# First weights of the first expert loaded through GpSimd's queue at step 16 and split in steps 17 to 19; four table scatters put behind tile 23's decayed queries

## The chip, the cores and the metric

The kernel runs on one core of a Trainium2 chip. The core has a matrix engine (TensorE, PE in the profile; PEld is its loading of weights), VectorE (DVE), ScalarE (ACT), GpSimd (POOL) and SyncE (SP, which only issues transfers), and 16 DMA engines that all queues share. Each engine works through its own instructions in program order and stops at an instruction whose semaphores are not yet there. The metric is the time of one execution in microseconds (us) on the device.

## What is computed

A retention layer over 4 batches, 8 heads, 768 positions and 64 channels a head, then a mixture of 8 experts with one expert for each token:

```python
for b in range(nb):                       # blocks of 64 positions, per batch and head
    intra = (qb @ kb.T * Dmask) @ vb      # Dmask: lam ** (i - j) below the diagonal
    inter = (qb * lam_pow) @ kv_state
    out[b] = intra + inter
    kv_state = lam_block * kv_state + (kb * rev_pow).T @ vb
x = out.transpose(0, 2, 1, 3).reshape(3072, 512)
e_idx = argmax(x @ w_gate)                # one expert of 8 for each token
h  = relu(x[mask] @ w1[e])                # 512 -> 1024, float32
ye = h @ w2[e]                            # 1024 -> 512
out[mask] = gate_w * sigmoid(x @ w_output_gate)[e] * ye
```

## The kernel before

**Attention.** The 3072 tokens are 24 tiles of 128 positions (6 chunks by 4 batches). A software pipeline runs over steps s = -2 to 21. Step s transposes the queries and keys of tile s+2 (`stage_a`: PSUM banks pk and pq, L341), applies the running state to the decayed queries of tile s (`stage_c1`, L424), makes the scores of tile s+1 (`stage_b`, L400) and multiplies the scores of tile s by its values and updates the state (`stage_c`, L441 and L454). ScalarE copies the transposed keys and queries out of PSUM (kT L344, qT L345) and the outputs (xT L448). VectorE applies the decay to the scores (L409), updates the state (L466) and turns the outputs for their store (xn L532). GpSimd makes the decayed queries (`stage_q`, qd, L375; in two halves for tiles 20 to 23) and decayed keys (kd, L316). All PSUM tiles share 8 banks, so a new tile of PSUM waits for the engine that reads the old tile of its bank.

**Routing.** For every four tiles logits are made, and for each token a record (row, scale) is scattered to a table in HBM by GpSimd, one indirect DMA for a tile (`place_scatter`, L679). In the last steps the order of GpSimd's work is written by hand in the dictionary `work`, whose three lists for a step are run between the halves of `stage_q`, ahead of the decayed keys, and behind them. The expert that is largest after 12 tiles is taken first; its rows of the first 12 tiles are gathered in steps 17 to 19 (`row`, L900). A later load of the table index (L834) waits until all scatters ahead of it have landed.

**Experts.** Float32 weights come in pieces of 1 MB (`load_piece`, L119, tile raw with 3 buffers, issued by SP) and are split in two parts: whi, a cast on ScalarE (`split_hi`, L132), and wlo, the rest, on VectorE (`split_lo2`, L146 for two quarters at once), for three matmuls per product (`mm3`, L85 to L87). Piece 0 is the first half of the first expert's w1. Behind the last step the program goes on with tiles 22 and 23, `keep_places`, the first expert's first columns (`x_hi`, `x_lo`), the logits of the last four tiles, and then `fill`, which runs matmuls of the first expert while the rest of its rows are still being routed. From about 144 us on the experts follow one another.

Of the kernel before, what the change touches and what calls it, by code (L numbers as in the profile page):

```python
# [23 lines left out]
def kernel(  # L24
# [13 lines left out]
    nc = tc.nc  # L38
# [37 lines left out]
    RES = 16  # L76
# [33 lines left out]
    def load_piece(i, eng=nc.sync, j=None):  # L110
        if i >= len(pieces):
            return
        p, m, s = pieces[i]
        src = (w1, w2)[m][bass.ds(expert[p], 1)]
        src = src[:, :, s * HALF : (s + 1) * HALF] if m == 0 else src[:, s * HALF : (s + 1) * HALF, :]
        if i not in raws:
            raws[i] = wpool.tile([P, 4, 512], F32, tag="raw", bufs=3, name=f"raw_{i}")
        c = slice(0, 4) if j is None else slice(j, j + 1)
        eng.dma_start(raws[i][:, c, :], src.rearrange("e (c p) f -> p (e c) f", p=P)[:, c, :])  # L119

    def split_hi(i, j):
        if i >= len(pieces):
            return
        if pieces[i] not in wparts:
            wparts[pieces[i]] = (
                wpool.tile([P, 4, 512], F32R, tag="whi", bufs=4, name=f"whi_{i}"),
                wpool.tile([P, 4, 512], F32R, tag="wlo", bufs=4, name=f"wlo_{i}"),
            )
        src, hi = raws[i][:, j, :], wparts[pieces[i]][0][:, j, :]
        if turned_out(i):  # L130
            src, hi = by_quarter(src), by_part(hi)
        nc.scalar.copy(out=hi, in_=src)  # L132
# [10 lines left out]
    def split_lo2(i, h):  # L143
        sl = slice(2 * h, 2 * h + 2)
        hi, lo = (t[:, sl, :] for t in wparts[pieces[i]])
        nc.vector.tensor_tensor(out=lo, in0=raws[i][:, sl, :], in1=hi.bitcast(F32), op=ALU.subtract)  # L146
# [149 lines left out]
    def blank_rows():  # L296
        norow = wpool.tile([P, E * EB * 3], I32, tag="raw", bufs=3, name="norow")
        nc.gpsimd.memset(norow, NOROW)
        nc.sync.dma_start(tab_d.rearrange("(p r) t -> p (r t)", p=P), norow)
# [132 lines left out]
    def stage_c(n):  # L432
        L = live[n]
        c, b = divmod(n, B)
        vt = qkv[n][2]
        xT = slot(f"xT_{n}")
        for y in range(2):
            po = L["po"][y]
            for m in range(4):
                i, j = divmod(m, 2)  # L440
                nc.tensor.matmul(  # L441
                    po[j * D : (j + 1) * D, i * P : (i + 1) * P],
                    vt[:, 4 * y + m, :],
                    L["at"][y][:, m, :],
                    start=(c == 0),
                    stop=(c == 0 or m >= 2),
                )
            nc.scalar.copy(out=xT[:, 256 * y : 256 * y + 256], in_=po[:, 0:256])  # L448
        L["xT"] = xTs[n] = xT
        if c < NCH - 1:  # L450
            pst = bank(f"pst_{n}")
            for m in range(4):
                for y in range(2):
                    nc.tensor.matmul(  # L454
                        pst[y * D : (y + 1) * D, m * D : (m + 1) * D],
                        L["kd"][:, 2 * m + y, :],
                        vt[:, 4 * y + m, :],
                        start=True,
                        stop=True,
                    )  # L460
            psv = pst[:, 0 : 4 * D].rearrange("p (m d) -> p m d", m=4)
            if c == 0:
                nc.vector.tensor_copy(out=state[b], in_=psv)
            else:
                for m in range(4):
                    nc.vector.scalar_tensor_tensor(  # L466
                        out=state[b][:, m], in0=state[b][:, m], scalar=qdec[:, m, P - 1 : P], in1=psv[:, m],
                        op0=ALU.mult, op1=ALU.add,
                    )
            weave()  # L470
            weave()
# [356 lines left out]
    def load_rows(p, j0=0, j1=None, eng=nc.sync):  # L828
        if p >= E:
            return  # L830
        n = (KT[p] if j1 is None else j1) - j0
        t = const.tile([32, 4, n, 3], I32, name=f"index_{p}_{j0}")
        src = tab_v[bass.ds(expert[p], 1)][:, :, j0 : j0 + n, :]
        eng.dma_start(t, src.rearrange("e (b r) j t -> (e r) b (j t)", b=4))  # L834
        idxs[(p, j0)] = (t, n)
# [381 lines left out]
    with tc.manual_schedule():  # L1217
# [12 lines left out]
        def row(b):  # L1230
            return lambda: gather(0, b, b + 1, RES0 * P)

        def rec():
# [5 lines left out]
            RES0: ([], [], []),  # L1239
            RES0 + 2: ([], [rec], [rec]),  # L1240
            RES0 + 3: ([], [rec], [rec, lambda: load_rows(0, 0, 2, nc.gpsimd)]),
            RES + 2: ([row(2)], [], [row(3)]),
            RES + 3: ([row(4)], [], [row(5)]),
            RES + 4: ([rec], [], [rec]),
            RES + 5: ([rec], [], [rec]),
        }
        between.update({(s, k): fs for s, w in work.items() for k, fs in zip(("q", "qk", "end"), w)})

        for s in range(-2, NTILE - 2):
            if s >= 0:  # L1250
                load_up_to(s + AHEAD - (4 <= s <= RES), 2 if s <= RES else 1)
            for i in range(3):
                if s == RES + (2, 4, 5)[i]:
                    load_piece(i)
            if s == -2:
                decay_table()
            if s == 0:
                stage_b(1)
                stage_b2(1)
            rest = stage_a(s + 2)  # L1260
            if late and s != RES + 5:
                late.pop(0)()
            if s >= 1 and s % B == 0:
                logits(s - B, B)
            for f in rest:
                f()
            if s >= 0:
                stage_c1(s)
            stage_a2(s + 2)
            if s == RES + 4:  # L1270
                stage_q(s + 2)
            if s + 1 >= 0 and s != 0:
                stage_b(s + 1)
            if s == RES + 5:
                late.pop(0)()
                seen = rank_counts("plater")
            n = s - 1
            if s >= 1 and s % B == 0:
                logit_rows(s - B)
            if n >= 0 and n % B == B - 1:  # L1280
                choice = route_choose(n + 1 - B, n + 1)
                ranking = route_place(n + 1 - B, n + 1)
                if s != RES + 4:
                    at_once(choice)
                    pace(uncounted[-1][0][0:1, 0, 0:1])
                per_turn[0] = 3 if n >= RES else 2
            if s == RES + 5:
                stage_d2(LAST)
            if s + 1 >= 0 and s != 0:
                stage_b2(s + 1)  # L1290
            stage_k(s + 2)
            if s == RES0 + 2:
                expert_regs(0, order_i, 1)
            if s == RES + 5:
                for f in held[:6]:
                    f()
                x_turn(0, 0)
            gap_work(s, "end")
            if s == RES + 4:
                at_once(choice[:-1])  # L1300
            if 0 <= n < LAST:
                stage_d2(n)
            if s == 0:
                later.extend(inter_tables())
                routing_tables()
                order_tables()
            if s == 1:
                weave(len(later))
            if s == 2:
                blank_rows()  # L1310
            if s >= 0:
                stage_c(s)
            if s == RES + 4:
                choice[-1]()
            if s == RES + 1:
                row_index(0)
                row(0)()
                row(1)()
            if ranking and s == RES + 4:
                late.append(ranking[0])  # L1320
                held = ranking[1:]
                ranking = []
            if ranking and s != RES0:
                late.append(ranking[0])
                later.extend(ranking[1:])
                ranking = []
            if ranking:
                for f in pick_first():
                    f()
                late.append(ranking[0])  # L1330
                later.extend(ranking[1:])
                ranking = []
            if s < RES0 - 2:
                place_scatter(1)

        n = NTILE - 1
        for j in range(2):
            split_hi(0, j)
        stage_c1(n - 1)
        stage_b(n)  # L1340
        stage_b2(n)
# [8 lines left out]
            x_hi(0, g, 0)  # L1350
        for g in range(NPAIR):
            x_lo(0, g, 0)
        split_lo2(0, 0)
        split_hi(0, 2)
        load_piece(3)
        stage_c1(n)
        stage_c(n)
        split_hi(0, 3)
        split_lo2(0, 1)
        for i in range(2):  # L1360
            rows_of(LAST + i)
        logits(LAST, B)
# [249 lines left out]
```

## Time and profile before

| | |
|---|---|
| median of 3 runs | 418.16 us (417.45 to 418.74) |
| the profiled execution | 415.14 us |
| its span, first to last instruction | 413.4 us |
| PE / PEld busy | 400.8 us (97%) / 367.1 us (89%) |
| DVE / POOL / ACT busy | 286.7 / 238.8 / 190.4 us |
| HBM traffic | 190 GB/s over the span |

The timeline gives for each group of instructions the start, the duration, the engine, the line, the operation with its tiles, and in brackets the idle time of the engine just before with what ended it. The windows give the busy time of each engine in a stretch, the granted clock of TensorE (1.00 is 2.4 GHz, 0.50 is 1.2 GHz), the busy share of the DMA engines, and GB/s. A DMA instruction's duration is its issue, not its transfer.

### The profile page before, as it was taken

To read this page: it belongs to the slowest core of one execution; us is meant where nothing else is said; L and a number is where in the kernel's file an instruction comes from. 1 tells how busy PE (TensorE), PEld (TensorE's weight loads), DVE (VectorE), ACT (ScalarE), POOL (GpSimd) and SP (SyncE) were. 2 spreads that over 40 slices of the span, in tenths; PEclk is the share of its full clock that TensorE was granted. 3 is DMA by queue.
4 is the path that set the end of the run, shared out by engine and by line. 5 is a ranking of instruction groups with operands and counts; after the bars stand their busy time and mean duration, and the time that the engine had idled before them with its cause. 6 is when DMAs were issued, how large, how long until landed. Compare 5 with 4: busy or idle time off the path is not lost.

```text
span 413.4 us, 10570 instructions
## 1 busy us (share of the span) xinstructions
PE 400.8 (97%) x3869; PEld 367.1 (89%) x3869; DVE 286.7 (69%) x810; ACT 190.4 (46%) x460; POOL 238.8 (58%) x301
## 2 busy tenths in 40 slices
PE   7999999999899999999999999999999999999994
PEld 4889878798698698999999999999999989989983
DVE  2759697877888646876868857957965864873710
ACT  4767665665684033544145325504704543542400
POOL 5367679668846788674783665467386266120012
PEclk9999999999999999999999999999999999999999
DMA  8999898889972764544479548746846884461001
GB/s 177 231 254 246 226 258 224 215 230 259 322 231 79 222 206 144 170 141 135 150 209 297 198 135 241 262 178 200 292 140 186 295 271 151 127 224 46 5 27 52
DMA packets 95103, 79.11 MB, mean 191 GB/s; under 512 B 58445, under 2 KB 70769, under 8 KB 95041
## 3 DMA queue, kind: packets, MB, share of 16 engines
q1 hardware_dynamic: 88080, 64.88, 53.2%
q0 software_dynamic: 6240, 12.93, 10.0%
q8 instruction: 32, 0.52, 0.5%
q10 hardware_dynamic: 720, 0.53, 0.5%
q14 instruction: 31, 0.25, 0.2%
HBM read 62.25 MB, written 16.45 MB: 190 GB/s over the span
## 4 chain that ended last, share of the span: by engine, by line
PE 85%; DVE 6%; DMA 5%; issue 2%; POOL 1%; ACT 0%; POOLq 0%; DVEq 0%; SPq 0%
PE ph_None L86 10%; PE ph_None L87 10%; PE ph_None L85 10%; PE py L87 6%; PE py L86 6%; PE py L85 6%; PE pyr L86 5%; PE pyr L87 5%; PE pyr L85 5%; PE ps L400 4%; PE po L441 4%; PE pk L341 3%; PE po L424 2%; PE pq L341 2%; DVE at L409 2%; PE pst L454 2%
## 5 line engine op out<-in xcount | busy, mean ns | idle before, releaser
L900 POOL DMA_INDIRECT xg<-x_d,rows x100 | 110.6, 1106 | 54.8 <-issue 28.9
L1009 ACT ACTIVATE hhi<-ph_None 128x400 fp32r<-128x400 f32 (+4 forms) x56 | 28.1, 501 | 115.8 <-PE ph_None L87 111.0
L86 PE MATMUL ph_None<-xlo,whi 128*128 128x400 f32 (+4 forms) x224 | 76.2, 340 | 0.0
L87 PE MATMUL ph_None<-xhi,wlo 128*128 128x400 f32 (+4 forms) x224 | 76.1, 340 | 0.0
L85 PE MATMUL ph_None<-xhi,whi 128*128 128x400 f32 (+4 forms) x224 | 76.1, 340 | 0.0
L132 ACT CAST whi<-raw 128x512 fp32r<-128x512 f32 x128 | 74.7, 615 | 2.4 <-DMA raw<-in_moe_w_dram 2.4
L141 DVE TENSOR_TENSOR wlo<-raw,whi 128x512 fp32r<-128x512 f32 x112 | 74.5, 686 | 0.7 <-ACT whi L132 0.5
L1010 DVE SCALAR_TENSOR_TENSOR hlo<-ph_None,hhi 128x400 fp32r<-128x400 f32 (+4 forms) x56 | 31.9, 570 | 35.2 <-ACT hhi L1009 33.2
L87 PE MATMUL py<-hhi,wlo 128*128 128x400 f32 (+2 forms) x128 | 44.4, 347 | 0.0
L86 PE MATMUL py<-hlo,whi 128*128 128x400 f32 (+2 forms) x128 | 44.4, 347 | 0.0
L85 PE MATMUL py<-hhi,whi 128*128 128x400 f32 (+2 forms) x128 | 44.4, 347 | 0.0
L86 PEld LDWEIGHTS ph_None<-xlo,whi 128*128 128x128 f32 x224 | 42.0, 188 | 0.5 <-DVE xlo L935 0.2
L1126 POOL DMA_INDIRECT out_dram<-yn,table x12 | 12.5, 1045 | 51.8 <-DVE yn L1190 34.6
L85 PEld LDWEIGHTS ph_None<-xhi,whi 128*128 128x128 f32 x224 | 42.0, 188 | 0.4
L87 PEld LDWEIGHTS ph_None<-xhi,wlo 128*128 128x128 f32 x224 | 42.0, 188 | 0.2
L345 ACT COPY qT<-pq 64x256 f32<-64x256 f32 x96 | 37.8, 393 | 2.0 <-PE pq L341 1.0
L409 DVE TENSOR_TENSOR at<-ps,decay 128x512 f32<-128x512 f32 x48 | 31.1, 681 | 10.4 <-PE ps L400 10.4
L86 PE MATMUL pyr<-wlo,hhi 128*128 128x512 f32 (+2 forms) x96 | 37.8, 394 | 0.5 <-DVE wlo L146 0.5
L87 PE MATMUL pyr<-whi,hlo 128*128 128x512 f32 (+2 forms) x96 | 37.6, 391 | 0.0
L85 PE MATMUL pyr<-whi,hhi 128*128 128x512 f32 (+2 forms) x96 | 37.5, 390 | 0.0
L931 ACT CAST xhi<-y 128x256 fp32r<-128x256 f32 (+3 forms) x64 | 19.5, 357 | 31.5 <-DVE y L917 31.5
L679 POOL DMA_INDIRECT tab_d<-rec,idx x24 | 26.2, 1090 | 10.0 <-issue 4.1
(216 smaller groups left out, 783.0 us busy)
## 6 DMA issues: line engine op xcount, KB each, us to landing
raw<-in_moe_w_dram SPq DMA_DIRECT2D x32, 1024.0 KB
x_d<-xn SPq DMA_DIRECT2D x22, 256.0 KB
qkv<-in_k_dram SPq DMA_DIRECT2D x40, 128.0 KB
qkv<-in_v_dram SPq DMA_DIRECT2D x20, 256.0 KB
qkv<-in_q_dram SPq DMA_DIRECT2D x36, 128.0 KB
yd<-yo SPq DMA_DIRECT2D x12, 256.0 KB
yr<-yd SPq DMA_DIRECT2D x48, 64.0 KB
xg<-x_d,rows POOLq DMA_INDIRECT x100
```

What stands on the lines that cost most here:

```text
L85: nc.tensor.matmul(ps, a[0], b[0], start=first, stop=False)
L86: nc.tensor.matmul(ps, a[0], b[1], start=False, stop=False)
L87: nc.tensor.matmul(ps, a[1], b[0], start=False, stop=last)
L132: nc.scalar.copy(out=hi, in_=src)
L141: eng.tensor_tensor(out=lo, in0=src, in1=hi.bitcast(F32), op=ALU.subtract)
L341: nc.tensor.transpose(out=dst[:, m * P : (m + 1) * P], in_=src[:, m], identity=ident)
L345: copies = [lambda r=r, view=view, src=src: nc.scalar.copy(out=view(qT[r]), in_=src) for r, view, src in query_parts(pq)]
L409: nc.vector.tensor_tensor(out=at, in0=ps.rearrange("p (g t) -> p g t", g=NPAIR), in1=dec[:, j], op=ALU.mult)
L679: nc.gpsimd.indirect_dma_start(out=tab_d, out_offset=bass.IndirectOffsetOnAxis(ap=idx, axis=0), in_=rec, in_offset=None, bounds_check=P * ...
L900: nc.gpsimd.indirect_dma_start(out=xg[(p, i)][:, m * P : (m + 1) * P], out_offset=None, in_=x_q[0 : 4 * rows], in_offset=bass.IndirectOffs ...
L1009: nc.scalar.activation(out=hi[:, r], in_=ph[:, r], func=AF.Relu)
L1010: nc.vector.scalar_tensor_tensor(out=lo[:, r], in0=ph[:, r], scalar=0.0, in1=hi[:, r].bitcast(F32), op0=ALU.max, op1=ALU.subtract,)
```

## The change

Piece 0 is no longer issued by SP at the start of step 18, but by GpSimd at the end of step 16. Its four casts and two subtractions, which stood behind the last step, now stand in steps 17 (quarter 0), 18 (quarter 1) and 19 (quarters 2 and 3 and both subtractions). The four scatters of the records of tiles 12 to 15, which stood between and behind the halves of the decayed queries of tiles 22 and 23, now all stand behind tile 23's. In the diff RES is 16.

```diff
+            RES: ([], [], [lambda: load_piece(0, nc.gpsimd)]),
             RES + 2: ([row(2)], [], [row(3)]),
             RES + 3: ([row(4)], [], [row(5)]),
-            RES + 4: ([rec], [], [rec]),
-            RES + 5: ([rec], [], [rec]),
+            RES + 5: ([], [], [rec] * 4),
...
-            for i in range(3):
+            for i in range(1, 3):
                 if s == RES + (2, 4, 5)[i]:
                     load_piece(i)
...
+            if s == RES + 3:
+                split_hi(0, 2)
             if s >= 0:
                 stage_c(s)
+            for j in {RES + 1: (0,), RES + 2: (1,), RES + 3: (3,)}.get(s, ()):
+                split_hi(0, j)
+            if s == RES + 3:
+                for h in range(2):
+                    split_lo2(0, h)
...
         n = NTILE - 1
-        for j in range(2):
-            split_hi(0, j)
...
-        split_lo2(0, 0)
-        split_hi(0, 2)
         load_piece(3)
         stage_c1(n)
         stage_c(n)
-        split_hi(0, 3)
-        split_lo2(0, 1)
```

On ScalarE, in steps 17 and 18, the rows stood as follows before (the number behind a name's letters is the tile, or the piece; the last number is the buffer's):

```order
L448 COPY xT_17_2076<-po_17_0_2027 128x256
L448 COPY xT_17_2076<-po_17_1_2028 128x256
L344 COPY kT_20_2137<-pk_20_2127 128x512
L345 COPY qT_20_2138<-pq_20_2128 64x256 x4
L448 COPY xT_18_2189<-po_18_0_2144 128x256
```

and in the changed kernel, with the cast of piece 0's first quarter ahead of tile 20's keys:

```order
L448 COPY xT_17_2078<-po_17_0_2029 128x256
L448 COPY xT_17_2078<-po_17_1_2030 128x256
L132 CAST whi_0_2106<-raw_0_1959 128x512
L344 COPY kT_20_2140<-pk_20_2130 128x512
L345 COPY qT_20_2141<-pq_20_2131 64x256 x4
L448 COPY xT_18_2192<-po_18_0_2147 128x256
L448 COPY xT_18_2192<-po_18_1_2148 128x256
L132 CAST whi_0_2106<-raw_0_1959 128x512
```

What moved: the casts came from behind tile 21's and tile 22's outputs to places ahead of the transposed keys and queries of tiles 20, 21 and 22, and the first of them is the first instruction that waits for the load.

On GpSimd, from the end of step 16 to tile 20's decayed queries, the changed kernel has:

```order
L375 TENSOR_TENSOR qd_18_1912<-qT_18_1877,qdec_132 128x512
L316 TENSOR_TENSOR kd_18_1913<-k_18_1660,kdec_130 128x512
L119 ISA
L119 DMA raw_0_1959<-in_moe_w1_dram 128x4x512
L375 TENSOR_TENSOR qd_19_2039<-qT_19_2017,qdec_132 128x512
L316 TENSOR_TENSOR kd_19_2045<-k_19_1764,kdec_130 128x512
L900 DMA xg_0_2116<-x_d_72,rows_0_0_2111 128x128 x2
```

The two rows of L119 are new there; the others keep their order.

On GpSimd at the end of the steps the rows were before, from tile 22's decayed queries on (kept in the buffer qkv_22_1):

```order
L375 TENSOR_TENSOR qkv_22_1_1995<-qT_22_2312,qdec_132 128x256
L679 DMA tab_d_73<-rec_12_1938,idx_12_1941 24576x3
L375 TENSOR_TENSOR qkv_22_1_1995<-qT_22_2312,qdec_132 128x256
L679 DMA tab_d_73<-rec_12_1938,idx_12_1941 24576x3
L571 IOTA rec_16_2376 128x4
L572 TENSOR_SCALAR rec_16_2376<-row0_138 128x4
L375 TENSOR_TENSOR qkv_23_1_2119<-qT_23_2424,qdec_132 128x256
L679 DMA tab_d_73<-rec_12_1938,idx_12_1941 24576x3
L375 TENSOR_TENSOR qkv_23_1_2119<-qT_23_2424,qdec_132 128x256
L679 DMA tab_d_73<-rec_12_1938,idx_12_1941 24576x3
L679 DMA tab_d_73<-rec_16_2376,idx_16_2379 24576x3 x4
```

and are now:

```order
L375 TENSOR_TENSOR qkv_22_1_1997<-qT_22_2320,qdec_132 128x256 x2
L571 IOTA rec_16_2381 128x4
L572 TENSOR_SCALAR rec_16_2381<-row0_138 128x4
L375 TENSOR_TENSOR qkv_23_1_2124<-qT_23_2426,qdec_132 128x256 x2
L679 DMA tab_d_73<-rec_12_1938,idx_12_1941 24576x3 x4
L679 DMA tab_d_73<-rec_16_2381,idx_16_2384 24576x3 x4
```

The scatters of tiles 12 to 15 (rec_12) moved behind both halves of tile 23, where they stand ahead of those of tiles 16 to 19 (rec_16).

## Rows read from the trace of the kernel before

**Rows 1.** Windows: length; busy PE, PEld, DVE, ACT, POOL; PEclk, DMA share, GB/s.

```profile
90.00:113.00 23.00, 21.11 (x451) 17.40 (x449) 19.23 (x67) 14.64 (x41) 20.13 (x24) 1.00 1.01 286
113.00:144.00 31.00, 30.50 (x251) 25.29 (x248) 24.21 (x76) 14.44 (x39) 20.22 (x20) 1.00 0.55 175
```

**Rows 2.** Timeline of POOL at the end of step 16.

```profile
88.10 0.63 POOL L834 DMA_DIRECT2D index<-tab_d  x1 [3.10 <-DMA tab_d<-rec,idx]
...
91.66 1.26 POOL L375 TENSOR_TENSOR qd<-qT,qdec 128x512 f32<-128x512 f32 x1
```

**Rows 3.** Timeline of ACT in step 17, and tile 20's copies.

```profile
89.26 0.81 ACT L448 COPY xT<-po 128x256 f32<-128x256 f32 x2 [0.54 <-PE po L441]
90.74 0.59 ACT L344 COPY kT<-pk 128x512 f32<-128x512 f32 x1 [0.67 <-PE pk L341]
91.23 1.63 ACT L345 COPY qT<-pq 64x256 f32<-64x256 f32 x4
```

**Rows 4.** Timeline of PE, steps 18 and 19; last row from step 21.

```profile
93.47 0.63 PE L454 MATMUL pst<-v,kd 128*64 128x64 f32 x16
...
94.52 0.60 PE L341 MATMUL pq<-ident,q 128*128 128x128 f32 x4
95.05 1.10 PE L424 MATMUL po<-qd,state 64*64 64x128 f32 x16
96.10 1.10 PE L400 MATMUL ps<-qT,kT 64*64 64x128 f32 x32
...
104.43 0.67 PE L424 MATMUL po<-qd,state 64*64 64x128 f32 x16
```

**Rows 5.** Timeline of POOL: a plain load of 512 rows that it issues.

```profile
2.44 0.96 POOL L215 DMA_DIRECT2D wgs<-in_moe_w_gate_dram  x1 [0.32 <-POOL wgs L214]
```

**Rows 6.** Timelines of POOL and DVE: a 3 KB index load from issue to use.

```profile
124.14 0.63 POOL L834 DMA_DIRECT2D index<-tab_d  x1 [4.10 <-DMA tab_d<-rec,idx]
...
126.82 0.16 DVE L869 SCALAR_TENSOR_TENSOR rowf<-index 32x8 f32<-32x8 int32 x1 [0.97 <-DMA index<-tab_d]
```

**Rows 7.** Windows (columns as in rows 1), then DMA queues from 92 to 99 us.

```profile
92.00:99.00 7.00, 6.99 (x147) 5.91 (x140) 6.79 (x23) 4.39 (x12) 5.48 (x6) 1.00 1.02 256
137.50:139.50 2.00, 2.00 (x9) 1.14 (x8) 0.73 (x2) 0.00 (x0) 1.39 (x2) 1.00 1.08 410
...
q1 hardware_dynamic: 4914, 1.70, 97.9%
```

**Rows 8.** Timelines of SP and ACT: piece 0, issue and first use.

```profile
101.14 0.41 SPq L119 DMA_DIRECT2D raw<-in_moe_w_dram  x1
...
110.11 1.14 ACT L132 CAST whi<-raw 128x512 fp32r<-128x512 f32 x2 [2.35 <-DMA raw<-in_moe_w_dram]
```

**Rows 9.** Timeline of PE: second halves of tiles 22 and 23.

```profile
108.04 0.45 PE L424 MATMUL po<-qkv,state 64*64 64x128 f32 x8 [0.32 <-POOL qkv L375]
...
112.38 0.45 PE L424 MATMUL po<-qkv,state 64*64 64x128 f32 x8 [1.53 <-POOL qkv L375]
```

**Rows 10.** Timeline of POOL: tile 23's second half, and scatters.

```profile
111.58 0.75 POOL L375 TENSOR_TENSOR qkv<-qT,qdec 128x256 f32<-128x256 f32 x1
...
119.08 0.97 POOL L679 DMA_INDIRECT tab_d<-rec,idx  x1 [0.30 <-issue]
```

**Rows 11.** Timeline of DVE: a gap in step 20, and piece 0's subtractions.

```profile
102.23 1.29 DVE L409 TENSOR_TENSOR at<-ps,decay 128x512 f32<-128x512 f32 x2 [2.28 <-PE ps L400]
...
114.31 2.36 DVE L146 TENSOR_TENSOR wlo<-raw,whi 128x1024 fp32r<-128x1024 f32 x2
```

**Rows 12.** Windows at the end, then PE's timeline at the start.

```profile
407.00:408.00 1.00, 0.45 (x4) 0.23 (x2) 0.48 (x1) 0.00 (x0) 0.00 (x0) 1.00 0.31 95
412.00:413.00 1.00, 0.00 (x0) 0.00 (x0) 0.00 (x0) 0.00 (x0) 0.00 (x0) 0.50 0.00 0
...
5.32 1.09 PE L341 MATMUL pk<-ident,qkv 128*128 128x128 f32 x4 [0.65 <-DMA qkv<-in_k_dram]
...
9.49 0.60 PE L341 MATMUL pq<-ident,qkv 128*128 128x128 f32 x4
```

## The prediction

> **What bounds it now.** I read the windows first. TensorE is busy in 97% of the span (the table above); between 90 and 113 us it is busy 21.11 of 23.00 us and from 113 to 144 us 30.50 of 31.00 [rows 1]. So it is the bound, and all that a change of waits can give back in the stretch that this one touches is 2.4 us of visible gaps. The reader should see in the same rows that the DMA engines are full until 113 us (share 1.01) and that GpSimd is busy 20.13 of 23 us. Next I read the timelines of each engine there. GpSimd runs behind the step that TensorE is in: step 16's last instruction on GpSimd, tile 18's decayed keys, ends as the next row begins, at 91.66, since the index load ahead of it had stood 3.10 us for its scatters [rows 2]. ScalarE is in step 17 at 89.26 to 90.07 and goes on with tile 20's keys at 90.74 [rows 3]. TensorE is about to enter step 19 at 94 us [rows 4]. "Step 16" on one engine and "step 17" on another are therefore not in the order of their numbers: ScalarE's end of step 17 comes ahead of GpSimd's end of step 16. The two gaps that the moved scatters can close are TensorE's waits for GpSimd's decayed queries, 0.32 and 1.53 us [rows 9].
>
> **The load, and when it lands (L).** GpSimd reaches it at 91.66 [rows 2]. A GpSimd load with as many rows (128 partitions by 4) took 0.96 us to issue [rows 5]: it ends at 92.62. The trace has no large load from GpSimd's queue, so I bound the rest. A 3 KB load was used 2.05 us after its issue ended (126.82 less 124.77) [rows 6]; that is the fixed part. 1,024 KB at the 410 GB/s that loads of weights reached when they had the DMA engines to themselves is 2.56 us [rows 7]: the lower bound is L = 97.2. But here the engines are full with SP's transfers (share 1.02 at only 256 GB/s [rows 7]). If the two queues got equal time the data would need 5.1 us, L = 99.8. I take a turn of one packet each: SP's 4,914 packets filled 97.9% of 16 engines for 7 us, 22 ns a packet [rows 7], while a 2 KB packet at 410 GB/s over 16 engines takes 80 ns, so piece 0 gets 78% of the time: 3.3 us, L = 98.0. I choose it because SP's packets are mostly small (1.70 MB in 4,914).
>
> A rule speaks to the same number: the Trainium skill, page "DMA: Bandwidth & Descriptors", section "Anatomy of one DMA — SWDGE (gpsimd) path", fits a GpSimd load as 2.0 us plus bytes over 436 GB/s from its start, 4.4 us for this one as an estimate, which would be L = 96.1 and a time of some 419.6; its fixed 2.0 us agrees with the 2.05 us of rows 6, and no run here shows it for a large load beside a full queue.
>
> **What waits for it.** The cast of quarter 0 stands on ScalarE directly behind tile 17's outputs, which end at 90.07 [rows 3], and ahead of tile 20's keys and queries. ScalarE executes in order, so it stands from 90.07 to L, 7.9 us. Queued behind: kT and qT of tile 20, xT of tile 18, and all that follows. TensorE waits for them early, because PSUM's 8 banks go round: tile 18's state product (pst) takes the bank that kT of tile 20 empties, and tile 21's queries (pq) the one that qT of tile 20 empties. After L come a cast (1.14 for two, 0.57 [rows 8]), kT (0.49 from start to start) and qT (1.63) [rows 3]:
> - pst of tile 18, at 93.47 before, starts at L + 1.2 = 99.2. TensorE has a pause of 5.7 us.
> - pq of tile 21, at 94.52 before, starts at L + 2.7 = 100.7, which is 6.2 us late. The state matmuls behind it took 1.10 us because of a wait for VectorE, and 0.67 where nothing held them [rows 4]; VectorE has caught up by then, so 0.4 us comes back. Scores of tile 20 are 5.7 us late (L less 92.3).
>
> GpSimd's work on tile 20's decayed queries needs qT as well, so it is late by about as much as TensorE and keeps its lead. SP's loads of tiles 22 and 23 lose up to the 3.3 us that piece 0 takes; TensorE is later than that, so I cost it at nothing. If the pause were not there, that loss could show.
>
> **What comes back.** The four scatters no longer stand ahead of the second halves of tiles 22 and 23: 0.32 + 1.53 = 1.85 us of waits go [rows 9]. They are hidden from then on behind the first expert's first matmuls. From the end of tile 23's second half (111.58 + 0.75) the last scatter ends after 7.7 us before (120.05), now after eight scatters at about 1.27 us, 10.2 us [rows 10]. With the query halves late by the same 5.7 us less the two scatters that stood between them, this chain is about as late as TensorE, and the index load behind it then finds emptier DMA engines; nothing, with 0 to +0.6 us as its bounds. The two subtractions on VectorE cost 2.36 us and lie in a gap like the 2.28 us one ahead of tile 21's scores [rows 11]: nothing; uncovered, 0.1 us. The three other casts (0.6 us each) lie in ScalarE's slack, 14.64 busy of 23 [rows 1]. Behind the last step, ScalarE and VectorE lose the same work, but TensorE's gaps there came from GpSimd. Of the 0.5 us of gaps after 113 us I count all as gone, since the other engines have time to catch up [rows 1]. In sum 2.35 us come back.
>
> **TensorE's clock.** At the end of the trace the granted clock is 1.00 in the microsecond of the last matmul, and 0.50 (1.2 GHz) at 412 to 413, with nothing run between [rows 12]. The pause here, 5.7 us, is longer than that idle time, so I expect the clock to be at the lower level when matmuls resume. What that costs: the first four transposes took 1.09 us, and 0.60 from 9.49 on [rows 12], so slow work costs as much again as it does at full clock. The slow stretch at the start lasted 4.2 us at most (9.49 less 5.32), so the loss lies between 0 and 2.1 us. I take 1.3, since TensorE is not yet kept full in the first microseconds.
>
> **Sum.** 5.7 - 1.85 - 0.5 + 1.3 = +4.7 us. It is made on the profiled execution of 415.14 us, which ran 3.0 us under the median of the runs; added to the median of 418.16 it is 422.9 us.
>
> **Rivals.**
> 1. The pause stays, but the clock holds: +3.4 us, 421.5. For it: no row shows a pause of this length in mid-kernel. Against: the rows at the end.
> 2. Piece 0 flows while its descriptors are still being written, unhindered by SP's queue: L = 91.66 + 2.05 + 2.56 = 96.3, a pause of only 4.0 us with no fall of the clock, and 96.3 - 92.3 - 2.35 = +1.7 us, 419.8. For it: the lower bound is 0.9 us away. Against: the DMA share of 1.02. The Trainium skill's fit quoted above would give nearly this.
> 3. GpSimd's queue gets what a load from SP got here: from the end of its issue at 101.55 to 110.11, 8.6 us [rows 8]. L = 101.2, and +6.6 us before the clock, 426 with it. Against: SP's load stood behind other loads of its own queue.
> 4. Faster: the load lands early enough for what comes back to outweigh it. At most 2.35 us, 415.8. It decides at L = 94.6, which is 2.0 us after the issue's end; 3 KB alone took 2.05 [rows 6]. Waits hidden inside busy rows, or GpSimd reaching the load earlier, would be needed.
> 5. The same: lateness and return cancel at L near 95 to 96, or TensorE takes back more than its visible gaps.
>
> **How the numbers follow.** Chances: forecast 0.46 (421.8 to 424.9), rival 1 0.20, rival 2 0.12, rival 3 0.08, rival 4 0.06, rival 5 0.08. About 0.3% (1.3 us) is what a measurement of this kernel can tell from no change. Slower by more: the forecast, rivals 1 and 3 and most of rival 2, 0.83; within it 0.11; faster 0.06. The range 419.0 to 425.8 reaches into rival 2 below and to equal time for both queues with a fallen clock above, and leaves out rival 4, most of 5 and most of 3.
>
> **What would show it.** In the changed profile: GpSimd's L119 within 0.5 us of 91.7, about 1 us long; ScalarE idle for some 8 us in front of the first L132, released by the DMA of raw; TensorE idle 5 to 6 us ahead of tile 18's L454; PEclk under 1.00 in the microseconds behind it; no wait of L424 for GpSimd's L375 in the last two tiles; the first matmuls of the experts proper (at about 144 us before) about 4 to 5 us later. It would be wrong if ScalarE's wait were under 6 us, if GpSimd came to its load several us before 91, or if the gap in TensorE were shorter than ScalarE's by more than the 3.4 us from 90.07 to 93.47.

## The result, and the profile after

The changed kernel takes 423.0 us (median of 6 runs, 421.57 to 425.49); the kernel before took 417.8 us on the same chip (6 runs, 415.38 to 419.76). The ratio is 1.013, with a 95% interval of 1.0083 to 1.0177: 1.3% slower, some 5.2 us. The profiled execution took 423.02 us with a span of 421.4.

The page's busy times and granted clock of the changed kernel (40 equal slices):

```profile
PE 401.4 (95%) x3869; PEld 367.9 (87%) x3869; DVE 286.9 (68%) x810; ACT 190.6 (45%) x460; POOL 239.3 (57%) x302
...
PEclk9999999997999999999999999999999999999997
```

TensorE is busy for 0.6 us more than before, in a span that is 8.0 us longer: most of the loss is idle time, and the tenth slice (95 to 105 us) is the only one in mid-kernel with a lower clock. The windows of the changed kernel, with columns as in [rows 1]:

```profile
90.00:113.00 23.00, 17.13 (x321) 14.69 (x313) 14.47 (x44) 11.12 (x28) 15.76 (x17) 0.85 1.03 277
...
99.00:100.00 1.00, 0.00 (x0) 0.00 (x0) 0.00 (x0) 0.00 (x0) 0.00 (x0) 0.87 1.24 287
...
105.00:106.00 1.00, 1.00 (x28) 1.00 (x24) 0.00 (x0) 0.98 (x3) 0.84 (x2) 0.50 1.05 301
106.00:107.00 1.00, 1.00 (x26) 0.83 (x20) 0.02 (x1) 0.63 (x2) 0.98 (x2) 0.72 1.20 292
107.00:108.00 1.00, 1.00 (x24) 1.00 (x25) 1.00 (x2) 0.37 (x1) 0.84 (x2) 1.00 0.84 229
```

TensorE does 17.13 us of work in the 23 us in which it did 21.11 [rows 1], with a clock of 0.85 on average. The clock falls to 0.50 (1.2 GHz) while TensorE stands, and is back between 106 and 107 us, after 5 us of work at the lower level. The timelines of GpSimd and ScalarE in the changed kernel:

```profile
92.13 0.84 POOL L119 DMA_DIRECT2D raw<-in_moe_w_dram  x1
...
102.79 0.72 POOL L375 TENSOR_TENSOR qd<-qT,qdec 128x256 f32<-128x256 f32 x1 [4.03 <-ACT qT L345]
...
90.80 0.81 ACT L448 COPY xT<-po 128x256 f32<-128x256 f32 x2 [0.57 <-PE po L441]
100.13 0.62 ACT L132 CAST whi<-raw 128x512 fp32r<-128x512 f32 x1 [8.52 <-DMA q<-in_q_dram]
```

The load is issued where [rows 2] put it, and ScalarE stands 8.52 us ahead of its first cast. The releaser named there is a load of q that ended at the same moment; the cast reads only raw, and in runs e7 and e8 below the same wait is put down to raw. TensorE in the changed kernel, from tile 18's products to the last logits:

```profile
94.89 1.09 PE L441 MATMUL po<-at,v 128*64 128x128 f32 x16 [0.18 <-DMA v<-in_v_dram]
101.38 1.12 PE L454 MATMUL pst<-v,kd 128*64 128x64 f32 x16 [5.39 <-ACT kT L344]
102.43 1.12 PE L341 MATMUL pk<-ident,k 128*128 128x128 f32 x4
...
105.24 1.70 PE L400 MATMUL ps<-qT,kT 64*64 64x128 f32 x32
106.86 1.09 PE L441 MATMUL po<-at,v 128*64 128x128 f32 x16
...
117.00 0.67 PE L424 MATMUL po<-qkv,state 64*64 64x128 f32 x16
...
119.49 0.67 PE L424 MATMUL po<-qkv,state 64*64 64x128 f32 x16
...
122.90 0.86 PE L501 MATMUL pl<-xT,wgs 128*32 128x128 f32 x24 [0.31 <-ACT xT L448]
```

The pause is 5.39 us, in front of tile 18's pst, and ScalarE's kT ends it. Behind it the transposes take 1.12 us where they took 0.66. The two waits of [rows 9] are gone. A small new one stands at the logits. The chain of work that ended last (start, duration, what) goes through the same place in the changed kernel, to the pst at 101.38:

```profile
92.63 7.52 DMA q<-in_q_dram
...
100.66 0.59 ACT kT L344
```

The DMA queues of the changed kernel from 93.0 to 100.1 us, between issue and use (q0 is GpSimd's queue, q1 SP's; packets, MB, share of 16 engines):

```profile
q1 hardware_dynamic: 2708, 1.02, 56.6%
q0 software_dynamic: 295, 1.10, 46.6%
```

The same view from 95 to 98 us, and then from 98 to 100.1 us:

```profile
q0 software_dynamic: 216, 0.85, 77.1%
q1 hardware_dynamic: 212, 0.12, 12.7%
...
q1 hardware_dynamic: 1328, 0.46, 91.7%
q0 software_dynamic: 65, 0.19, 26.5%
```

Over the 7.1 us GpSimd's queue had 46.6% of the time of the 16 engines, but not evenly. It moved 0.06 MB before 95 us, then 0.85 MB in three us, packet for packet with SP's queue (216 to 212) and with 77.1% of the time. Behind 98 us it had 26.5% beside SP's 91.7%. Some of its packets are those of two gathers, issued at 96.31 and 97.75 us.

### The profile page after: what moved, and what is told of

Read it like the earlier page. It is cut to its first block, busy times and chain, and to the rows that moved or that the text cites. A ratio compares the mean times of both kernels' runs of the same rounds, so it can differ in the third digit from the quotient of the medians.

```text
span 421.4 us, 10574 instructions
## 1 busy us (share of the span) xinstructions
PE 401.4 (95%) x3869; PEld 367.9 (87%) x3869; DVE 286.9 (68%) x810; ACT 190.6 (45%) x460; POOL 239.3 (57%) x302
## 4 chain that ended last, share of the span: by engine, by line
PE 84%; DMA 8%; DVE 3%; SPq 1%; ACT 1%; issue 1%; POOL 0%; POOLq 0%; DVEq 0%; ACTq 0%
PE ph_None L86 9%; PE ph_None L87 9%; PE ph_None L85 9%; PE py L86 6%; PE py L85 6%; PE py L87 6%; PE pyr L86 5%; PE pyr L87 5%; PE pyr L85 5%; PE ps L400 3%; PE po L441 3%; DMA qkv<-in_k_dram 2%; PE pk L341 2%; DMA qkv<-in_q_dram 2%; PE pq L341 2%; DMA q<-in_q_dram 2%
## 5 line engine op out<-in xcount | busy, mean ns | idle before, releaser
L375 POOL TENSOR_TENSOR qkv<-qT,qdec 128x512 f32<-128x512 f32 (+1 forms) x18 | 20.8, 1162 | 18.3 <-ACT qT L345 8.2
```

What stands on the lines that cost most here:

```text
L375: nc.gpsimd.tensor_tensor(out=live[n]["qd"][:, g], in0=live[n]["qT"][:, g], in1=qdec[:, g], op=ALU.mult)
```

## The experiments

**Theory:** the loss is ScalarE's stand in front of the load, which TensorE shares (its pause and the lower clock behind it), less what the moved scatters give back. **Rivals:** the load takes the DMA engines from SP's loads of keys and queries; the moved casts and subtractions take the time of ScalarE and VectorE wherever they stand. Each run has its own median of the kernel before on its chip; 1% is 4.2 us.

### e1: only the scatters moved

```diff
 (kernel before)
-            RES + 4: ([rec], [], [rec]),
-            RES + 5: ([rec], [], [rec]),
+            RES + 5: ([], [], [rec] * 4),
```

> The kernel before, with only the four table scatters moved behind tile 23's decayed queries. My theory (the loss of the changed kernel is ScalarE standing in front of its first cast until GpSimd's load has landed, plus the lower clock after the pause; the moved scatters by themselves are a gain): the 0.32 and 1.53 us waits of TensorE's L424 for GpSimd's L375 go, 1.5 to 2.4 us faster than before, ratio 0.994 to 0.997. Rival (the scatters only move the wait: the last scatter, the index load behind it and the first expert's late rows come 2 to 3 us later, and TensorE waits there): L424's waits go, but a wait of 1 to 2 us appears between 130 and 145 us, ratio 0.999 to 1.003.

Measured: 417.8 us, ratio 1.0013 (0.9977 to 1.0049). A gain of 1.85 us would be 0.9956, which the interval excludes. TensorE in e1 behind the last tile:

```profile
114.12 1.06 PE L501 MATMUL pl<-xT,wgs 128*32 128x128 f32 x26 [0.83 <-ACT xT L448]
...
116.05 0.33 PE L511 MATMUL pl<-ident,lT 128*128 128x128 f32 x1 [0.28 <-ACT lT L505]
```

The waits at L424 are gone, but the logits now wait for ScalarE's copy of tile 23's outputs. The first matmul of the fill starts at 116.57 us and started at 116.83 before, so 0.26 us is left of 1.85. The ratio is the rival's, but the wait isn't where the rival had it: from 120 to 144 us TensorE is busy for 24.00 of 24 us.

### e2: load and scatters moved, casts and subtractions at their old place

```diff
 (changed kernel)
-            if s == RES + 3:
-                split_hi(0, 2)
...
-            for j in {RES + 1: (0,), RES + 2: (1,), RES + 3: (3,)}.get(s, ()):
-                split_hi(0, j)
-            if s == RES + 3:
-                for h in range(2):
-                    split_lo2(0, h)
...
+        for j in range(2):
+            split_hi(0, j)
...
+        split_lo2(0, 0)
+        split_hi(0, 2)
...
+        split_hi(0, 3)
+        split_lo2(0, 1)
```

> The changed kernel with the casts and subtractions of piece 0 back behind the last step; the load stays on GpSimd at step 16. My theory: nothing waits for the load in steps 17 to 19, so no pause, no fall of the clock, and the gain of the scatters stays: 1 to 2.4 us faster than before, ratio 0.994 to 0.998. Rival (the early load itself costs: it takes the shared DMA engines from SP's loads of tiles 21 to 23, and TensorE waits for those): TensorE shows waits on transfers of k, q or v of 2 to 4 us between 95 and 107 us, ratio 1.000 to 1.008. Rival (the split work crowds the steps): as mine.

Measured: 418.5 us, ratio 1.0004 (0.9974 to 1.0034). No pause, and a clock of 1.00 from 90 to 113 us. TensorE in e2 waits for SP's loads instead; of four such waits, together 2.42 us, the longest is:

```profile
110.60 0.67 PE L341 MATMUL pq<-ident,qkv 128*128 128x128 f32 x4 [1.09 <-DMA qkv<-in_q_dram]
```

Moving the casts and subtractions away, with the load left in place, removes the whole loss. The rival of the full DMA engines may be seen in the rows, but not in the time; and such waits also stand where GpSimd loads no weights (0.93 and 1.61 us at 36 and 42 us in e11).

### e3: load at step 15, casts and subtractions where the change put them

```diff
 (changed kernel)
-            RES0 + 3: ([], [rec], [rec, lambda: load_rows(0, 0, 2, nc.gpsimd)]),
-            RES: ([], [], [lambda: load_piece(0, nc.gpsimd)]),
+            RES0 + 3: ([], [lambda: load_piece(0, nc.gpsimd), rec], [rec, lambda: load_rows(0, 0, 2, nc.gpsimd)]),
```

> The changed kernel with GpSimd's load one step earlier, at step 15 ahead of a scatter and ahead of the index load that made GpSimd late, so some 10 us sooner (issue near 82, landing near 90); casts stay in steps 17 to 19. My theory: ScalarE's wait at the first cast is under 1 us, TensorE has no pause above 1 us there and the clock stays at 1.00: 0.5 to 2.4 us faster than before, ratio 0.994 to 0.999. Rival (split work in steps 17 to 19 crowds ScalarE and VectorE, whatever the load does): ratio 1.004 or more, with no single long wait. Rival (the early load takes the DMA engines): ratio 1.002 to 1.010, TensorE waiting for k, q or v.

Measured: 418.0 us, ratio 1.0023 (0.9989 to 1.0056). No pause for kT. The longest wait of TensorE in e3, and the microsecond ahead of it, in which TensorE stood:

```profile
89.41 0.44 PE L341 MATMUL pq<-ident,q 128*128 128x128 f32 x2 [1.69 <-DMA q<-in_q_dram]
```

```profile
88.00:89.00 1.00, 0.00 (x0) 0.00 (x0) 1.00 (x5) 0.12 (x1) 0.00 (x0) 1.00 1.18 330
```

So the casts and subtractions in steps 17 to 19 cost nothing that can be measured, once their data is there. From both sides, e2 and e3, the loss is the meeting of the two: a cast that comes to ScalarE ahead of its load. Both medians lie above the theory's ranges (0.998 and 0.999 at most); the gain that it counted on from the moved scatters doesn't show, as in e1.

### e4 and e4b: TensorE kept at work in the pause

```diff
 (changed kernel, stage_c; e4 had the same behind the loop over y, with L["po"][1])
+            if n == RES + 2 and y == 1:
+                for _ in range(44):
+                    nc.tensor.matmul(po[:, 256:512], blank[:, 0:P], blank[:, 0:256], start=True, stop=True)
             nc.scalar.copy(out=xT[:, 256 * y : 256 * y + 256], in_=po[:, 0:256])
```

> The changed kernel with 44 extra matmuls (128x256 bf16, into unused columns of tile 18's output bank) in front of tile 18's state product, so that TensorE works through some 5 us of the time in which ScalarE stands; their results are not used. If the lower clock costs 2 us, as the changed kernel's rows suggest (5.5 us from tile 18's state product to tile 19's values at the lower level against 3.7): the granted clock stays at 1.00 and the time is 1.5 to 2.5 us under the changed kernel's, ratio to before 1.006 to 1.010. If the clock costs nothing, because the other engines set the pace behind the pause: the same as the changed kernel, ratio 1.012 to 1.014.

e4 measured: 430.5 us, ratio 1.0293 (1.0251 to 1.0336). It doesn't do what it was meant to. TensorE in e4:

```profile
104.61 6.32 PE L452 MATMUL po<-blank 128*128 128x256 bf16 x44 [9.36 <-ACT xT L448]
```

The added matmuls write to the bank that ScalarE still had to copy, so they stood behind the pause and lengthened it. In e4b they stand ahead of that copy:

> The changed kernel, with 44 matmuls (128x256, result unused) that depend on no transfer, behind the products of tile 18 and ahead of ScalarE's copy of the second of them, so that TensorE runs them inside its pause of 5.4 us (at full clock they take 4.7 us, 44 x 256 columns at 2.4 GHz). Theory: the pause costs in two ways, 5.4 us of standing and a lower clock behind it (0.50 to about 106.5 us), which costs some 2.2 us. With the pause filled, the granted clock stays near 1.00, the state product of tile 18 still starts at about 101.4 us, and the time falls by about 2 us against the changed kernel: a ratio of 1.007 to 1.009 to the kernel before. Rival: the work behind the pause is held by transfers or ScalarE and not by the clock; then the ratio stays at 1.012 to 1.014 though the clock shows 1.00.

e4b measured: 421.5 us, ratio 1.0089 (1.006 to 1.0118). TensorE in e4b, and windows behind its wait:

```profile
104.45 0.69 PE L457 MATMUL pst<-v,kd 128*64 128x64 f32 x16 [3.97 <-ACT kT L344]
```

```profile
105.00:106.00 1.00, 1.00 (x10) 0.58 (x6) 0.82 (x4) 0.96 (x3) 0.13 (x1) 0.72 0.82 200
106.00:107.00 1.00, 1.00 (x8) 0.67 (x12) 0.03 (x1) 1.00 (x4) 0.84 (x2) 0.50 0.71 214
107.00:108.00 1.00, 1.00 (x20) 1.00 (x24) 0.00 (x0) 0.99 (x3) 0.97 (x2) 0.50 1.12 282
108.00:109.00 1.00, 1.00 (x31) 1.00 (x28) 0.00 (x0) 0.95 (x4) 0.84 (x2) 0.57 0.86 277
```

The profiled execution, 426.1 us, is the longest of the twelve, and the load took 8.5 us to land in it (94.75 to 103.20). So 3.97 us of wait were left, and the clock, which the theory had near 1.00, was low for some 3.4 us (by the granted clock of these windows). In the changed kernel it was low for some 6.8 us, with TensorE at work in 5.2 of them. The ratio is where the theory put it, 1.7 us under the changed kernel's, but the two intervals overlap, and this trace is not that of a middle execution: the run doesn't show the price of the clock. Rows of other runs do, for the stretch behind the pause. TensorE at tile 18's pst and at tile 19's products in e4, and then in e8 (below):

```profile
110.86 0.69 PE L457 MATMUL pst<-v,kd 128*64 128x64 f32 x16
...
113.97 1.09 PE L441 MATMUL po<-at,v 128*64 128x128 f32 x16
...
101.65 1.12 PE L454 MATMUL pst<-v,kd 128*64 128x64 f32 x16 [6.34 <-ACT kT L344]
...
106.28 1.09 PE L441 MATMUL po<-at,v 128*64 128x128 f32 x16
```

The same work took 3.11 us in e4, behind a longer stand but with a clock of 1.00 (110 to 114 us). It took 4.63 us in e8 and 4.78 in e6, each with some 3.4 us of it at the lower clock, and 5.48 in the changed kernel, with 5.2. What this is worth at the end of the kernel no run shows by itself.

### e5 and e9: the casts two steps later

```diff
 (changed kernel; e9 has the casts so too, and split_lo2 where it stood before)
-            if s == RES + 3:
+            if s == RES + 5:
                 split_hi(0, 2)
...
-            for j in {RES + 1: (0,), RES + 2: (1,), RES + 3: (3,)}.get(s, ()):
+            for j in {RES + 3: (0,), RES + 4: (1,), RES + 5: (3,)}.get(s, ()):
...
-            if s == RES + 3:
+            if s == RES + 5:
```

> The changed kernel with the four casts and two subtractions two steps later (steps 19, 20 and 21 in place of 17, 18 and 19); the load stays where it is. Theory (ScalarE's stand in front of the first cast is the whole loss): the cast comes to ScalarE at about 102 us, after the landing at about 100; no wait of TensorE over 1.2 us between 90 and 113 us that goes back to ScalarE, clock 0.99 or more, ratio 0.997 to 1.003. First rival: the casts among the last steps delay the transposed keys and queries by their own length, whenever they stand there: waits of TensorE for kT or qT of some 0.6 us in three steps, ratio 1.004 to 1.006. Second rival: with the casts out of the way by 113 us, ScalarE copies the outputs of tile 23 in time, the waits at the logits of the last tiles go, and the time falls by about 1 us under before: ratio 0.996 to 0.998.

e5 measured: 419.8 us, ratio 1.0067 (1.0031 to 1.0103). No pause for kT, but none of the three expectations is quite right. VectorE and TensorE in e5 at tile 23, and its windows there:

```profile
113.98 2.32 DVE L146 TENSOR_TENSOR wlo<-raw,whi 128x1024 fp32r<-128x1024 f32 x2
116.21 1.28 DVE L409 TENSOR_TENSOR at<-ps,decay 128x512 f32<-128x512 f32 x2
...
116.95 1.72 PE L441 MATMUL po<-at,qkv 128*64 128x128 f32 x16 [2.07 <-DVE at L409]
118.60 1.97 PE L948 MATMUL pt<-ident,xT 128*128 128x128 f32 x8
```

```profile
117.00:118.00 1.00, 1.00 (x12) 0.82 (x14) 0.93 (x6) 0.00 (x0) 0.30 (x1) 0.67 1.06 401
118.00:119.00 1.00, 1.00 (x10) 0.67 (x7) 0.90 (x6) 0.55 (x3) 0.00 (x0) 0.50 1.10 341
```

Both subtractions now stand ahead of the decay of tile 23's scores, which no later tile covers. TensorE waits 2.07 us, and the clock falls behind that wait too: L441 takes 1.72 us in place of 1.09 and the transposes 1.97 in place of 1.09, another 1.5 us.

> The changed kernel with the four casts two steps later (19, 20, 21) and the two subtractions back behind tile 23's decay, where they stood before. In the run with both two steps later (ratio 1.0067) TensorE waited 2.07 us for VectorE's decay of tile 23, ahead of which one subtraction stood (2.32 us), and the clock fell behind that wait. Theory: that subtraction is what was left of the loss; the wait and the fall of the clock go, ratio 0.998 to 1.003. Rival: the load's share of the DMA engines is the rest (1.28 us of wait for tile 23's queries), whatever the subtractions do: ratio 1.004 to 1.007.

e9 measured: 418.2 us, ratio 1.0042 (1.0014 to 1.0071). The wait for the decay is gone, and no window around it has a lower clock. What is left lies between the two expectations. TensorE's longest wait in e9 is for a load:

```profile
100.67 0.63 PE L341 MATMUL pk<-ident,qkv 128*128 128x128 f32 x4 [1.26 <-DMA qkv<-in_k_dram]
```

e2, with the same load and such waits too, is at 1.0004, so whether the load's share of the engines costs 0 or 1.5 us stays open.

### e6 and e7: the load in four parts, and one step later

```diff
 (changed kernel, e6 and then e7)
-            RES: ([], [], [lambda: load_piece(0, nc.gpsimd)]),
+            RES: ([], [], [lambda j=j: load_piece(0, nc.gpsimd, j) for j in range(4)]),
...
-            RES: ([], [], [lambda: load_piece(0, nc.gpsimd)]),
+            RES + 1: ([], [], [lambda: load_piece(0, nc.gpsimd)]),
```

> The changed kernel with GpSimd's load issued in four parts of 256 KB, so that the first cast waits for one of them alone. Theory one, the landing is mostly time for data beside SP's full queue: of the 7.1 us from the end of issue to use, 2.05 are fixed and 5.05 go with the size, so the first quarter can be used some 3.3 us after its own issue, at about 96.2 us; ScalarE stands 4.6 us in place of 8.5, TensorE pauses 1.5 us and keeps its clock, ratio 1.000 to 1.004. Theory two, a GpSimd load waits its turn behind what SP has already queued, whatever its size: the first quarter comes at 99 to 100, the pause stays at 4.5 us or more, ratio 1.010 to 1.013. In both, GpSimd spends up to 2.9 us more on issues (3 x 0.96 at most), which may hold back the decayed queries of tile 19: a wait of TensorE at L424 or of VectorE would show it.

e6 measured: 419.2 us, ratio 1.0044 (1.0015 to 1.0074). GpSimd, ScalarE and TensorE in e6:

```profile
94.20 2.23 POOL L119 DMA_DIRECT2D raw<-in_moe_w_dram  x4
...
99.02 0.62 ACT L132 CAST whi<-raw 128x512 fp32r<-128x512 f32 x1 [6.92 <-DMA v<-in_v_dram]
...
100.27 0.69 PE L454 MATMUL pst<-v,kd 128*64 128x64 f32 x16 [4.40 <-ACT kT L344]
```

The first quarter's issue ends at about 94.76 (a quarter of 2.23), and it is used 4.26 us later, where the whole megabyte took 7.16 (92.97 to 100.13). So a good part of the landing goes with the size: 2.9 us came off, where theory one had 3.8 and theory two nothing. The pause was still 4.40 us, because GpSimd came to the load 2.1 us later in this execution than in the changed kernel's (94.20 for 92.13) while TensorE was only 0.1 us later in step 18 (L424 at 93.30 for 93.17). The clock fell behind this pause too (0.50 from 102 to 104 us), which theory one had not. The ratio lies just above theory one's range and clear of theory two's; the profiled execution (420.46 us) took 1.2 us more than the median.

> The changed kernel with the load one step later, at the end of step 17 on GpSimd, about 3 us later (behind the decayed queries and keys of tile 19). Theory: the loss follows the landing one for one once TensorE is out of other work: the landing comes at about 103.2 us, ScalarE stands some 11.5 us, TensorE pauses about 8.5 us, the cost of the clock stays near 2.2 us, and the time is 3 us above the changed kernel: ratio 1.019 to 1.022. Rival: the transfers of SP catch up meanwhile and the load lands faster, 5 us after its issue; then the landing is at about 101.2 and the ratio 1.014 to 1.017.

e7 measured: 425.1 us, ratio 1.0189 (1.0142 to 1.0236). GpSimd, ScalarE and TensorE in e7:

```profile
93.73 0.84 POOL L119 DMA_DIRECT2D raw<-in_moe_w_dram  x1
...
102.29 0.62 ACT L132 CAST whi<-raw 128x512 fp32r<-128x512 f32 x1 [13.07 <-DMA raw<-in_moe_w_dram]
...
103.44 1.12 PE L341 MATMUL pq<-ident,q 128*128 128x128 f32 x4 [7.62 <-ACT kT L344]
```

A later load costs more, by about as much as it is later: 7.9 us over the kernel before, 2.5 us over the changed one, with a landing of 7.7 us (94.57 to 102.29) and no faster one as the rival had it. The interval reaches into the rival's range.

### e8: the change without the scatters

```diff
 (changed kernel)
-            RES + 5: ([], [], [rec] * 4),
+            RES + 4: ([rec], [], [rec]),
+            RES + 5: ([rec], [], [rec]),
```

> The changed kernel with the four scatters left where they stood before (between and behind the halves of the decayed queries of tiles 22 and 23): the load and the splits of the change alone. Theory as predicted: the moved scatters give 1.85 us back, so without them TensorE waits again for GpSimd's second halves (0.3 and 1.5 us at L424) and the time is 1.85 us above the changed kernel, ratio 1.016 to 1.019. Rival, from the run with the scatters alone (ratio 1.0013): the wait only moves to the logits of the last tiles, where tile 23's outputs are copied late; then the waits at L424 come back, the one at the logits goes, and the ratio stays at 1.011 to 1.015.

Measured: 421.2 us, ratio 1.0131 (1.0074 to 1.0188), the changed kernel's own. GpSimd and then TensorE in e8:

```profile
103.06 0.73 POOL L375 TENSOR_TENSOR qd<-qT,qdec 128x256 f32<-128x256 f32 x1 [2.78 <-ACT qT L345]
...
116.46 0.73 POOL L375 TENSOR_TENSOR qkv<-qT,qdec 128x256 f32<-128x256 f32 x1 [0.38 <-ACT qT L345]
...
118.91 0.77 PE L424 MATMUL po<-qkv,state 64*64 64x128 f32 x16
```

The median is the rival's, though the interval reaches the theory's 1.016 to 1.019. The mechanism of neither is in the rows: no wait at L424 came back though the scatters stand between the halves again. TensorE's L424 takes 0.77 us for all 16, where [rows 9] had a wait of 1.53. During ScalarE's stand GpSimd had gone on with gathers that don't need ScalarE, so that at tile 23 it waits for the queries (0.38 us) and no longer works off a backlog. From tile 19's products to tile 23's TensorE takes 13.33 us in e8 (106.28 to 119.61), 13.23 in the changed kernel and 15.62 before. The pause itself took the waits of [rows 9] away.

### e10 and e11: tile 23's outputs ahead of the first columns

```diff
 (e10 from e3, e11 from e1)
-        for g in range(NPAIR):
-            x_hi(0, g, 0)
-        for g in range(NPAIR):
-            x_lo(0, g, 0)
...
         stage_c1(n)
         stage_c(n)
+        for g in range(NPAIR):
+            x_hi(0, g, 0)
+        for g in range(NPAIR):
+            x_lo(0, g, 0)
```

> The kernel with the load at step 15 (no stand of ScalarE, ratio 1.0023), with the first expert's first columns (x_hi, x_lo) put behind tile 23's outputs, so that ScalarE copies these outputs first. Theory: the wait of 1.00 us at the logits goes, since ScalarE reaches that copy some 1.1 to 2.6 us earlier (the casts of x_hi take 1.1 and waited 1.5 for VectorE), and nothing takes its place, for the columns are used 4 us later: 1 us less, ratio 0.998 to 1.001. Rival: the columns are then late for the first expert's matmuls in the fill, or VectorE's queue is, and the wait only moves on: ratio 1.001 to 1.004.

> The kernel before with only the scatters moved (ratio 1.0013), with x_hi and x_lo put behind tile 23's outputs as well. Theory: the gain of 1.85 us that the moved scatters should give was taken back by the waits at the logits (0.83 and 0.28 us) for ScalarE's late copy; with that copy first the waits go and the time comes under the kernel before by 1 to 2 us: ratio 0.995 to 0.998. Rival: it is taken back again behind the logits (by the first columns, or by the routing chain of the last tiles, which sets when the fill ends): ratio 0.999 to 1.002.

Measured: e10 417.7 us, ratio 1.0038 (0.9994 to 1.0081); e11 416.8 us, ratio 1.0011 (0.9978 to 1.0044). TensorE behind the last tile in e10, and then in e11:

```profile
121.00 0.33 PE L511 MATMUL pl<-ident,lT 128*128 128x128 f32 x1 [0.82 <-ACT lT L505]
```

```profile
118.55 0.33 PE L511 MATMUL pl<-ident,lT 128*128 128x128 f32 x1 [0.51 <-ACT lT L505]
```

The wait at L501 is gone in both, and a wait stands one instruction further, at the transposed logits. Both medians lie in the rivals' ranges, and both intervals reach the theories': that the stretch behind the last tile gives the gain back fits the rows and isn't shown by the times. No version here is shown to beat the kernel before.

## Why the prediction was right, and where

**The kernel got slower by the pause: right, and shown.** 422.9 us was forecast and 423.0 measured. That they agree to 0.1 us is luck: the forecast is 4.7 us on top of a median of three runs (418.16), the measured rise is 5.2 on top of one of six (417.8), and terms of the sum err both ways. e2 and e3 each take away one side of the meeting between cast and load, and the loss goes; e7 makes the load later, and the loss grows with it.

**The landing: mis-sized.** GpSimd's load is at 92.13 (91.66 forecast) and takes 0.84 us to issue (0.96). From the end of the issue to the use it took 7.16 us, and 5.4 were forecast. The term that was mis-sized is the sharing of the DMA engines, which was taken to hold until the load is done. A turn for each packet was to give GpSimd's queue 78% of the time, and from 95 to 98 us it had 77.1%. But by 98.0, the forecast landing, at most 0.91 of the load's 1.05 MB had moved; the rest came while the queue had 26.5%, and took 2 us more. What cut its share there is not shown. The bound that I set aside, equal time for both queues (7.2 us), gives the total, though neither stretch has equal time. In e7 it was 7.7 us, and in e8 5.9 (94.49 to 100.40). The Trainium skill's fit, page "DMA: Bandwidth & Descriptors", section "Anatomy of one DMA — SWDGE (gpsimd) path", would have had 4.4 us from the start of the issue, as an estimate; here it took 8.0. The prediction set the fit's fixed 2.0 us, which it counts from the start of the issue, beside the 2.05 us of [rows 6], which count from its end; from the start that small load took 2.68 us (124.14 to 126.82).

**The pause: 5.39 us for 5.7 forecast, with two errors that cancel.** The load landed later than forecast by 2.1 us (100.13 for 98.0). But TensorE was 2.5 us late when it came to pst (95.99 for 93.47): the profiled execution was 1.5 us behind the one of before already in step 17 (L424 at 88.63 for 87.09), ahead of anything that the change touches, and lost 1.0 more in steps 17 and 18. Counted from step 17, pst is 6.4 us late (7.91 less 1.54), for 5.7 forecast.

**The clock: right in kind, mis-sized.** From pst to tile 19's products it takes 5.48 us (101.38 to 106.86), and took 3.67 before (93.47 to 97.14), 0.43 of it the wait in L424's 1.10 us [rows 4]. With TensorE busy in all of the 5.48 us, the lower clock cost about 2.2 us there, for 1.3 forecast and 2.1 as its bound. Rival 1, that the clock holds, fell.

**What comes back: right in size, wrong in cause.** From tile 19's products to tile 23's TensorE regains 2.4 us (106.86 for 97.14, then 120.09 for 112.76), for 2.35 forecast. The prediction gave 1.85 of that to the moved scatters and said that GpSimd "keeps its lead". e8's rows show that it comes back without them (2.3 us, 15.62 less 13.33), because the pause lets GpSimd catch up; e1 shows that without the pause the moved scatters give nothing that lasts. That the eight scatters and the later index load cost nothing fits e1 and e8.

**The casts, and the subtractions "in a gap": right for steps 17 to 19,** by e3. e5 shows what cover they had: at step 21 the same subtractions cost 2.07 us and a fall of the clock.

**SP's loads at nothing: right here, under the pause.** The prediction said that the loss could show without it. e2, e3 and e9 show such waits, 0.3 to 1.7 us each; the three ratios lie from 1.0004 to 1.0042, and what the waits cost in the end is not settled. Nor is it shown that GpSimd's load causes them: in e5 and e8 waits of 0.68 and 0.53 us for a load of q stand more than 5 us ahead of its issue.

**The sum.** The terms as measured are 6.4 + 1.8 - 2.4 = 5.8 us at tile 23 (1.8 is 5.48 less 3.67); the profiled pair ends 6.5 us apart after the 1.5, and the medians 5.2. Behind tile 23 the changed kernel regains 0.3 us until the experts proper start, and loses 0.9 in them; why was not followed. Of the signs named, one missed: the experts proper start 7.1 us later (151.25 for 144.18), 5.5 counted from step 17, where 4 to 5 were named.

## What to carry to other kernels

An early load is no help if its first reader stands in an in-order engine ahead of work that others wait for: place the reader by the worst landing, or leave it behind. Price such a load to its last bytes and not by its mean share: from the end of the issue to the use, the same megabyte took 5.9 to 8.0 us in the changed kernel, e7, e8 and e9. A visible wait of the bounding engine is worth its length only if what stands next to it is not about to become the limit: undo that part alone and look at the next wait.

## What the runs showed of the hardware that I had not expected

GpSimd's queue had no fixed share of the DMA engines beside SP's: 77.1% with 216 packets to SP's 212 (95 to 98 us), then 26.5% with 65 to 1,328. The first stretch is in e8 and e7 as well: 83.1% with 247 packets to 283 (96 to 99 us), and 83.5% with 217 to 442 (97 to 100 us). A fall of TensorE's clock doesn't need a pause as long as the change's: in e5 a wait of 2.07 us was followed by 0.50 and cost 1.5 us more, while waits of 1.53 us in the kernel before [rows 9] and 1.69 us in e3 had 1.00 around them. The clock can also fall when the work is back: in e6 the wait ends at 100.27, and the granted clock is 1.00 from 100 to 101 us and 0.56 in the next.
